# The down product of the last two chunks by seven half-size products, with an order of its own for the last chunk and its stores over two queues

## The chip, the cores and the metric

The kernel runs on one core of one Trainium2 chip. The metric is the device time of one execution in microseconds, the median of several runs; lower is better.

## What is computed

The reference runs a recurrent attention block ("rwkv7 goose") over 4 batches of 8 heads, 768 time steps and 40 channels, and hands its output, 3072 tokens of 320 features, to a feed-forward block:

```
y[t] = r[t] @ state
state = state * w[t] - outer(state @ a[t], b[t]) + outer(v[t], k[t])
...
h = x @ w_in                                  # 3072 x 320 by 320 x 2048
g = h * (1.0 / (1.0 + np.exp(-1.702 * h)))
return g @ w_out                              # 3072 x 2048 by 2048 x 320
```

All of it is float32. The change lies in the last line, the down product `g @ w_out`, and only in the part of it that belongs to the last 512 of the 3072 tokens.

## The kernel before

The 768 time steps are cut into 12 chunks of 64. A chunk has two units, one for each pair of batches, so there are 24 units of 128 tokens. For each unit the recurrence runs in a chunked form: cumulative decays (`ps_cum`, `ps_cumc`), a triangular system whose inverse is built in levels (`ps_N`, `ps_level`, `ps_Q`, `ps_T`), its solution (`ps_B`, `ps_X`), and the outputs and the new state (`ps_y`, then `zr`, and `x` by `decayed`). The unit's output `x` is written to a DRAM tile (`x_dram`, `part_with`) and read back in another layout (`xT_all`, `get_back`).

When both units of a chunk are there, `mlp(c)` runs the feed-forward block on the chunk's 256 tokens:

- **Up** (`up`, tiles `ps_up`): four groups q, each of 2048/4 = 512 hidden features. A group is 10 tasks of four matmuls with 256 columns.
- **Gelu** (`gelu`): one ScalarE instruction for each group, from a PSUM pair of banks into a tile `g`. Four `g` tiles exist.
- **Down** (`down(p)`, tiles `ps_down`): for each of the chunk's two units, 8 tasks `part(m)` of eight matmuls with 320 columns. The 64 tokens of a batch are the stationary operand, rows of `w_out` the moving one. Each half of the hidden features adds up in a bank of its own, so the result is a copy of one bank into `ob` and then an addition of the other (128 x 320 each), and after that two stores on SP's queue, one for each batch.

Every matmul takes a 64 x 64 quarter of the array; four quarters are issued in turn (`QUARTERS`). A float32 matmul of the program shows as two instructions in the profile. All matmuls carry the line of the helper `mm` (L300 in the profile of before), so they are told apart by tile.

The order is written out by hand, as one string `ORDER`. `plan.add` collects 2700 tasks, each with the engines it may run on, what it reads and writes, and for PSUM work a pair of banks. `ORDER` lists them: `2697d2` is task 2697 on VectorE with bank pair 2; p is TensorE, a ScalarE, d VectorE, g GpSimd, s a DMA on SP's queue. Four bank pairs exist. Each engine runs its own tasks in the listed order and waits where a task's inputs are not there. The recurrence of later chunks is woven between the up and down tasks of earlier ones, and the list ends with the up and down tasks of chunk 11 alone.

Of the kernel before, what the change touches and what calls it, by code (L numbers as in the profile page):

```python
# [58 lines left out]
class Plan:  # L59
# [29 lines left out]
    def listed(self, text):  # L89

        assert len(text.split()) == len(self.tasks)
        table, out, done = "exp", [], set()
        for one in text.split():
            e = next(e for e in ENGINES if ENGINES[e] in one)
            n, bank = one.split(ENGINES[e])
            t = self.tasks[int(n)]
            assert e in t.engines and t.after <= done and (e == "SP" or (t.pair is None) == (not bank))
            t.engine, t.bank = e, int(bank or 0)
            if e == "ACT" and t.table:
                t.load, table = t.table != table, t.table  # L100
            done.add(t)
            out.append(t)
        return out
# [4 lines left out]
0s 8s 26s 5s 7s 9s 3a 6s 87p0 88p1 24s 89a1 1s 2s 12s 102a 95d 100p2 90a0 93d 158a 101d2 98p3 96g 10s 94d 17s 97g 16s 99d3  # L108
103p1 4a 11s 132p0 104a1 105d1 142p2 143p3 133a0 106d 130p1 14s 144a3 13s 107p0 15s 18s 151g 108a0 109d0 51s 131a1 110p3 27s
149g 150d 111a3 112d3 159p0 156p1 145a2 161d0 160a0 152g 113p3 345s 92a 162d 25s 153d 114a3 163p2 42s 115d3 34s 19a 274s 264p0  # L110
165d2 265p3 164a2 22d 266a3 166p2 20d 273s 21d 33s 43s 167a2 154p3 168d2 23g 35s 28a 157d1 116p2 155d3 169p1 117a2 118d2 267a0
279d 63s 280g 119p3 277s 171d1 36s 44s 123a3 120d3 343s 125d3 121a 278g 124d3 29d 287a 126p2 170a1 288p0 127a2 30d 172p1 479s
122a3 31d 289a0 128p2 54s 173a1 45s 129d2 32g 62s 174d1 134p3 37a 290d0 175p2 344s 135d3 180a2 146s 178a2 275s 176d2 136p1
179a2 38d 181a2 39d 177a 282g 276s 291d 91s 138a1 182p0 188p3 281d 183a0 186p2 139d 137a1 283p0 187a2 184p1 189a3 40d 140s
292p2 46a 60s 284d0 41g 285p3 185d1 148a 286d3 190p0 293a2 294d2 334p1 335p3 357a 191d0 141s 268g 147s 336a3 315d 192p2 47d
337a1 348d 316p0 194a2 346s 295p3 349d 61s 317a0 195g 347s 358p1 296a3 297d3 360d1 318a0 298p3 271a 361d 319p0 338g 300d3 196s
193a2 320a0 355p2 385d 270s 48d 299a3 362p0 356d2 351g 301p3 363a0 364d0 350g 386p2 197s 302d3 365p0 387a2 269s 352g 359a1
303d3 388a2 323p1 367d0 366a0 321p3 49d 324a1 304p2 322a3 478s 325d1 50g 353p0 309a2 470p3 354d0 209p1 307a2 210p1 310a2 305d2
211p1 308a2 272d 198p0 341a 199p0 72s 212p1 70s 64a 200p0 340s 368p2 52s 342d 339s 69s 201p0 369a2 202p0 370d2 203p0 471a
213p1 65d 214p1 389p2 66d 472a3 483g 204p0 390a2 560s 371p3 67d 306a 53s 215p1 71s 482s 216p1 372a3 217p1 476a 220p2 373d3 68g  # L120
218p1 221p2 477d 219a1 205p0 222p2 206p0 223p2 224p2 78s 559s 207p0 55a 311p3 225p2 79s 312d3 80s 226p2 208a0 58d 313p1 374p3
314d1 227p2 56d 379a3 228p2 229p2 57d 326p0 230a2 59g 393p1 327d0 378a3 391p2 394a1 375d3 231p0 558s 392d2 376a 232p0 233p0
395d1 81s 73a 234p0 480s 381p2 235p0 474s 328p1 475s 382a2 74d 377a3 485d 380a3 236p0 75d 481s 492a 242p2 486d 243p2 82a 76d
484d 77g 383p3 237p0 384d3 244p2 329d1 330d1 488p3 473d 238p0 531d 245p2 487g 246p2 489d3 85d 532p1 708s 239p0 533a1 396p3
331d 534a1 240p0 247p2 397d3 332s 241a0 562s 535p1 83d 490p3 536a1 84d 398p0 706s 572a 491d3 86g 550p1 253p3 399d0 551a 555s
400d0 561s 333s 254p3 401d 255p3 552a1 564d 493p0 402s 556a 567g 570p1 554s 494d0 248p2 705s 563d 566g 249p2 495d0 498d 256p3
571d1 565g 403s 250a2 496a0 251d2 696p1 497g 557d 539p0 252s 537p2 257p3 538a2 704s 540d0 701s 258p3 553d 611d 697a 499d 573p2
259p3 576a2 574d2 784s 710d 700s 260p3 787s 541d0 575d2 404p0 578d 261a3 577g 405p0 579d 698a1 568p2 711g 500p1 406p0 569d2
501a1 407p0 262d3 580p2 702a 502d1 263s 408p0 582d2 409p0 503d 410p0 583d 504a 612p3 411p0 584g 613d3 412p0 614d3 413p0 505p1
709d 414a0 426p3 506d1 427p3 428p3 507d1 429p3 699d 581d2 430p3 615p1 703d 431p3 616a1 785s 585p0 432p3 508d 586a0 433p3 587d0  # L130
434p3 509a 588d 435p3 589d 448p2 436a3 510p1 590p0 511a1 449p2 592d0 591a0 512d1 415p3 513d 416p3 593d 514a 417p3 594g 418p3
515p0 419p3 516a0 517d0 595p1 518d 420p3 596a1 597d1 421p3 598d 422p3 519a 599d 423p3 424p3 520p0 425a3 437p1 521d0 438p1
523d0 522g 439p1 524d0 440p1 525d0 441p1 442p1 526d0 527p3 718p0 528a3 443p1 719d0 929s 444p1 720d0 529p3 445p1 721d0 446p1
530d3 600p0 723d 447a1 542p3 722d 724g 603d0 605a0 619p1 604d0 543d3 450p2 620a1 606d0 544p3 621d1 601d0 602d 617p1 707s 546d3
451p2 618a1 783s 712d 547g 713d 607p0 725p1 608a0 452p2 609p0 453p2 548s 610d0 932s 454p2 727d1 726d1 622p0 728d 545d3 729a
775p1 455p2 623d0 780s 776a 549s 756d 730p3 624p0 456d2 457d2 731d3 458s 459p2 777a1 778g 732d3 786s 788g 781a 779s 626d0
460p2 625d0 627g 733d 795p1 835d 734a 461p2 735p3 791g 462p2 628s 736a3 796d1 737d3 716p0 792g 738d 463p2 782d 739g 1011s
920p1 757p3 925s 464p2 717d0 758a3 629s 759a3 790d 465p2 740p0 789d 466p2 741a0 742d0 921a 797p3 467d2 760p0 1008s 468d2 800a3
923d 652p2 469s 761d0 922a1 653p2 926a 930s 798d3 714p1 799d3 654p2 924s 802d 801g 655p2 934d 803a 656p2 836p0 657p2 715d1
658p2 659p2 837d0 762p3 838d0 927d 660p2 763a3 661p2 764p1 662a2 743d 630p0 744d 928s 631p0 632p0 765d1 804p3 766d1 633p0  # L140
805a3 806d3 634p0 807d 635p0 808a 745p2 636p0 748d2 637p0 749d2 839p1 933g 750d2 638p0 840a1 1009s 751d2 639p0 809p3 746d2
935g 640a0 641p1 810d3 642p1 793p2 747a 811d3 674p0 812d 794d2 813a 752p3 643p1 753a3 814p2 644p1 815a2 816d2 754p3 645p1
755d3 646p1 817d 647p1 818a 767p2 841p3 768d2 648p1 842a3 649p1 819p2 650p1 820a2 821d2 769p3 822d 651a1 823d 675p0 771d3 931s
770d3 772g 824p2 936d 676p0 827a2 828a2 942p1 829a2 677p0 1153s 830a2 937d 945a1 773s 663p3 825d2 664p3 943d1 1156s 826a 665p3
944d1 999p2 947d 946g 666p3 1000a 1004s 980d 940p1 948g 667p3 941d1 668p3 774s 669p3 670p3 831p1 671p3 1001a2 1002d 1003s
832d1 672p3 1005a 1013d 678p0 673a3 1006d 833p2 843p1 679p0 834d2 1007s 844d1 938p2 845d1 680p0 939d2 846p3 681p0 847d3 949p1
# [102 lines left out]
def rwkv7_gelu_quick(ctx: ExitStack, tc: tile.TileContext, time_d, v_d, w_d, wc_d, ak_d, b_d, rv_d, w_in, w_out, out):  # L249
    nc = tc.nc  # L250
# [879 lines left out]
```

## Time and profile before

| | us |
|---|---|
| median of 3 runs | 679.55 (676.51 to 680.0) |
| the profiled execution | 682.79 |
| its span | 681.1 |
| what lies around its span | 1.7 |
| TensorE busy in the span | 652.0 |
| VectorE, ScalarE, GpSimd busy | 445.5, 330.7, 176.7 |

The profile's page gives each engine's busy time. The view of windows gives it by stretch, the view of waits says what an engine stood idle for, the chain of waits follows back what ended last, and the timeline lists instructions in order of time, merged where they are alike: start, length from the first start to the last end, engine, line, operation, tiles, shape and count. A matmul's own length (0.38 us for 256 columns) is a latency; several are in flight, so their pace is read from the starts of neighbouring groups.

### The profile page before, as it was taken

Reading aid. Unit: us, or ns where it says so; the run is one execution under the profiler, and the core shown is the slowest. Engines: PE = TensorE matmul, PEld = TensorE weight load, DVE = VectorE, ACT = ScalarE, POOL = GpSimd, SP = SyncE. Lnnn points to the kernel's source line nnn. Section 1 sums busy time; section 2 is a strip of 40 time slices with the busy share of each in tenths; the row PEclk is TensorE's granted clock in tenths of the full one; section 3 lists DMA queues with packets and bytes.
Section 4 is the critical chain, followed back from the end, with each engine's and each line's share of the span. In section 5 each row is a group of like instructions: output and inputs, shape, how many; then the busy total and the mean of one; then the engine's idle time right before and its main releaser. Section 6 shows DMA issues by size and latency. Waiting matters only on the chain.

```text
span 681.1 us, 42181 instructions
## 1 busy us (share of the span) xinstructions
PE 652.0 (96%) x19488; PEld 572.4 (84%) x19488; DVE 445.5 (65%) x906; ACT 330.7 (49%) x688; POOL 176.7 (26%) x204
## 2 busy tenths in 40 slices
PE   5777999999999999999999999999999999999997
PEld 5667888997987788888888898899899799889996
DVE  4687877777867668767776587868556766675001
ACT  4675845544564654664545445455454354252110
POOL 5443444225123123123123211321412421300000
PEclk9788999999999999999999999999999999999999
DMA  7874755205314314432404413513502312200100
GB/s 235 275 244 148 228 158 173 89 14 155 108 50 139 103 45 125 124 108 67 121 23 131 140 34 107 154 33 106 149 29 71 121 51 58 58 13 23 51 12 21
DMA packets 35312, 69.73 MB, mean 102 GB/s; under 512 B 5440, under 2 KB 14656, under 8 KB 35136
## 3 DMA queue, kind: packets, MB, share of 16 engines
q1 hardware_dynamic: 35136, 67.03, 32.8%
q8 instruction: 153, 2.51, 1.6%
q14 instruction: 23, 0.19, 0.1%
HBM read 59.15 MB, written 7.86 MB: 98 GB/s over the span
## 4 chain that ended last, share of the span: by engine, by line
PE 91%; DMA 4%; ACT 1%; DVE 1%; issue 1%; SPq 0%; ACTq 0%; DVEq 0%
PE ps_up L300 31%; PE ps_down L300 30%; PE ps_level L300 9%; PE ps_y L300 5%; PE ps_B L300 4%; PE ps_X L300 2%; PE ps_N L300 2%; PE ps_rz L300 2%; PE ps_RV L300 2%; PE ps_A L300 1%; DMA ak<-in_ak 1%; PE ps_zT L300 1%; PE ps_Q L300 1%; DMA time<-in_time 1%; PE ps_T L300 1%
## 5 line engine op out<-in xcount | busy, mean ns | idle before, releaser
L300 PE MATMUL ps_up<-xT_all,w_sb 64*64 64x256 f32 x3840 | 254.4, 377 | 2.0 <-DMA xT_all<-x_dram 1.1
L300 PE MATMUL ps_down<-w_sb,g 64*64 64x320 f32 x3072 | 240.3, 430 | 1.1 <-issue 0.9
L300 PEld LDWEIGHTS ps_up<-xT_all,w_sb 64*64 64x64 f32 x3840 | 172.9, 133 | 17.7 <-issue 2.5
L300 PEld LDWEIGHTS ps_down<-w_sb,g 64*64 64x64 f32 x3072 | 143.3, 133 | 31.4 <-issue 1.6
L988 ACT ACTIVATE g<-ps_up 128x1024 f32<-128x1024 f32 x48 | 49.1, 1024 | 44.7 <-PE ps_up L300 44.3
L709 POOL TENSOR_TENSOR EX<-ES,quads 128x512 f32<-128x512 f32 x29 | 38.3, 1323 | 115.5 <-DVE ES L702 83.1
L751 ACT COPY W<-ps_level 128x512 f32<-128x512 f32 x56 | 32.7, 585 | 69.1 <-PE ps_level L300 67.4
L300 PEld LDWEIGHTS ps_level<-W,EX 64*64 64x64 f32 x2560 | 59.2, 134 | 5.8 <-DVE T L830 0.2
L300 PE MATMUL ps_level<-W,EX 64*64 64x64 f32 (+1 forms) x2560 | 56.2, 217 | 0.0
L753 DVE TENSOR_TENSOR E<-two,ps_level 128x256 f32<-128x256 f32 x80 | 33.1, 415 | 34.7 <-ACT W L751 30.7
L707 ACT ACTIVATE EX<-ES,quads 128x256 f32<-128x256 f32 x80 | 36.3, 501 | 30.4 <-DVE ES L702 29.9
L619 POOL TENSOR_TENSOR ak<-ak,FT 128x512 f32<-128x512 f32 x16 | 22.0, 1378 | 76.2 <-DMA ak<-in_ak 54.4
L300 PE MATMUL ps_level<-PT,EX 64*64 64x64 f32 (+2 forms) x1280 | 34.9, 244 | 5.7 <-DVE EX L723 4.8
L300 PEld LDWEIGHTS ps_level<-PT,EX 64*64 64x64 f32 x1280 | 32.6, 145 | 8.9 <-DVE EX L723 5.7
L702 DVE STREAM_TRANSPOSE ES<-E 128x256 f32<-128x256 f32 x80 | 35.2, 442 | 4.7 <-DVE E L753 0.5
L300 PE MATMUL ps_y<-M,bh 64*64 64x104 f32 (+1 forms) x768 | 34.8, 247 | 1.3 <-DVE M L907 0.8
L300 PE MATMUL ps_y<-RV,kh 64*64 64x104 f32 (+1 forms) x768 | 34.9, 247 | 0.3 <-DVE EX L723 0.3
L891 ACT COPY B<-ps_B 128x416 f32<-128x416 f32 (+1 forms) x34 | 16.5, 492 | 33.5 <-PE ps_B L300 33.2
L300 PEld LDWEIGHTS ps_y<-RV,kh 64*64 64x64 f32 x768 | 28.9, 133 | 2.0 <-DVE M L907 0.5
L907 DVE TENSOR_TENSOR M<-ps_X,later 128x832 f32<-128x832 f32 (+1 forms) x24 | 23.8, 993 | 9.8 <-PE ps_X L300 9.5
L627 POOL TENSOR_TENSOR kh<-time,G 128x320 f32<-128x320 f32 x18 | 16.2, 902 | 48.4 <-PE ps_y L300 34.4
L300 PEld LDWEIGHTS ps_y<-M,bh 64*64 64x64 f32 x768 | 27.0, 133 | 1.9 <-DVE M L907 1.2
(131 smaller groups left out, 1097.2 us busy)
## 6 DMA issues: line engine op xcount, KB each, us to landing
ak<-in_ak SPq DMA_DIRECT2D x48, 160.0 KB
rv<-in_rv SPq DMA_DIRECT2D x48, 160.0 KB
time<-in_time SPq DMA_DIRECT2D x24, 320.0 KB
xT_all<-x_dram SPq DMA_DIRECT2D x48, 160.0 KB
wc<-in_wc SPq DMA_DIRECT2D x20, 264.0 KB
logw<-in_w SPq DMA_DIRECT2D x24, 160.0 KB
RV<-in_v SPq DMA_DIRECT2D x24, 160.0 KB
b<-in_b SPq DMA_DIRECT2D x48, 80.0 KB
```

The costliest lines, as they stand in the source:

```text
L300: nc.tensor.matmul(o, lhsT, rhs, start=start, stop=True, skip_group_check=True)
L619: plan.add(R, {"DVE": 690.0, "POOL": 1270.0, "sbuf": True}, lambda t: of(t.engine).tensor_mul(ahT(), ahT(), FT_of(i)), reads=T("ak", "FT") ...
L627: plan.add(R + 4, {"POOL": 870.0, "DVE": 490.0, "sbuf": True}, lambda t, n=n, dst=dst: of(t.engine).tensor_mul(dst(i)[:, :, :D], by_head(t ...
L702: plan.add(rank, dve(256), lambda t: nc.vector.transpose(ES(n), source(t)), writes=[key("ES", n, 6)], **reads)
L707: nc.scalar.activation(dst[:, :, h], ES(n), ACT.Copy, scale=quads[:, h, :1])
L709: of(t.engine).tensor_mul(dst, ES(n).unsqueeze(2).to_broadcast([128, 8, 2, 32]), quads.unsqueeze(1).to_broadcast([128, 8, 2, 32]))
L751: plan.add(rank, any2(512), lambda t: copy(t.engine)(tiles_of(W(n + 1)), blocks(psum(t, ""), 64)), writes=[key("W", n + 1, 5)], pair=pair)
L753: plan.add(rank, dve(256), lambda t: nc.vector.tensor_sub(tiles_of(E(n + 1)), every(two32, [128, 2, 4, 32]), blocks(psum(t, ""), 64)[:, :, ...
L891: plan.add(R, any2(4 * wide), lambda t: copy(t.engine)(dst(), some(psum(t, "")[:, :, :208])), writes=[("Bv", i)] if x and c > 0 else T("B" ...
L907: plan.add(R + 1, dve(8 * wide), lambda t: nc.vector.tensor_tensor(M_of(i)[:, :, :wide].rearrange("p (j b) n -> p b j n", b=2), some(psum( ...
L988: plan.add(-45, {"ACT": 1030.0, "table": "gelu"}, lambda t: nc.scalar.activation(g_of(c * NQ + q).rearrange("p m r n -> p r m n"), psum(t, ...
```

## The change

For chunks 10 and 11, `down` is replaced by `fast_down`. The product of a chunk, 256 tokens by 2048 features by 320 outputs, is seen as 2 x 2 blocks: the two units' tokens (p), two halves of the hidden features (s), and two halves of 160 outputs (d). Seven products of blocks take the place of eight, with sums before and after them (Strassen's scheme in Winograd's form):

- `factors()`: four combinations T1 to T4 of the blocks of `w_out`, made once, in two parts each (8 instructions of 128 x 640). They lie in `extra`, the staging tile of the weights.
- `mixed`: four combinations S1 to S4 of the blocks of `g`, in two parts each (8 instructions of 128 x 512 for a chunk), S2 to S4 partly in place of `g`.
- `product_of`: M1 to M7, each in two parts (j) of sixteen matmuls with 160 columns.
- `summed` and `added`: the banks are copied and added into SBUF (160, 320 or 480 columns wide), and combined into the four blocks of the result.
- Chunk 11 has its own order: M1 first, M2 last of all, added in PSUM onto M1, and the store of each block as soon as it is there. Of each pair of its stores one is issued on SP's queue and one on ScalarE's.

Beside this, `g` has six tiles in place of four, and its layout is [2, 4, 128] in place of [2, 2, 256] for all chunks, with the gelu's access patterns to match (the same 1024 elements). A scratch size of the DMA set-up is made smaller. The list `ORDER` is another one: 2736 tasks. Task by task, TensorE's order is the same in both lists for its first 651 tasks, SP's for its first 200, ScalarE's for 297, VectorE's for 512, GpSimd's for 88 (where the first `factors` tasks stand); from there all five differ. Some tasks before that have another bank pair. In number TensorE has 4 tasks fewer, ScalarE 10 fewer, VectorE 33 more, GpSimd 16 more and SP 1 more; in the last chunk all added arithmetic is on VectorE.

The diff without the list and without blank lines:

```diff
+            if e == "SP":
+                t.window = t.bank
...
+    FAST = (10, 11)
...
-                     ... x=1, xT=3, g=4, ob=1), 4)
+                     ... x=1, xT=3, g=6, ob=1, S10=1, S11=1, of=1, n6=1, n7=1), 4)
...
-    g_of = lambda n: buf("g", n, [128, 2, 2, 256])
+    g_of = lambda n: buf("g", n, [128, 2, 4, 128])
...
+    DH = DM // 2
+    S1 = single("S1", [128, 2, 4, 128])
+    T1, T2, T3, T4 = (extra[:, k * PIECE:(k + 1) * PIECE].rearrange("p (j f n) -> p j f n", j=2, f=4) for k in range(4))
+    B11, B12, B21, B22 = (w_out_sb.rearrange("p (j s f d n) -> p j s f d n", j=2, s=2, f=4, d=2)[:, :, s, :, d] for s in BITS for d in BITS)
+    of_fast, new6, new7 = (single(name, [128, n, DH]) for name, n in (("of_fast", 4), ("new6", 3), ("new7", 2)))
+    def light(n):
+        return {"POOL": 270.0 + 2.1 * n, "DVE": 165.0 + 1.03 * n, "sbuf": True}
+    def factors():
+        staged = [("weight", n) for n in range(len(raws))]
+        for dst, a, b, name, reads in ((T1, B12, B11, "T1", staged), (T2, B22, T1, "T2", [("T1", 0)]),
+                                       (T3, B22, B12, "T3", staged), (T4, B21, T2, "T4", [("T2", 0)])):
+            for j in BITS:
+                plan.add(10000, light(640), lambda t, dst=dst, a=a, b=b, j=j: of(t.engine).tensor_sub(dst[:, j], a[:, j], b[:, j]),
+                         reads=reads, writes=[(name, 0)])
+    def fast_down(c):
+        R = 10000 + 100 * c
+        last = c == NU // 2 - 1
+        A11, A21, A12, A22 = (lambda j, s=s, p=p: g_of(c * NQ + 2 * j + s)[:, p] for s in BITS for p in BITS)
+        g = lambda j, *which: [("g", c * NQ + 2 * j + s) for s in which]
+        T = lambda *names: [(name, c) for name in names]
+        s1 = lambda j: S1[:, j]
+        def mixed(j, name, dst, a, b, reads, writes, add=False):
+            def go(t):
+                (of(t.engine).tensor_add if add else of(t.engine).tensor_sub)(dst(j), a(j), b(j))
+            plan.add(-44, light(512), go, reads=reads, writes=writes + [(f"{name}{j}", c)])
+        def product_of(pair, n, at, a, b, j, reads, first=True):
+            def go(t):
+                po = psum(t, "ps_fast")
+                for f in range(4):
+                    for r, h in QUARTERS:
+                        mm(po[HALF[h], r, at * DH:(at + 1) * DH], a(j)[HALF[r], 2 * (f % 2) + f // 2, h * 64:h * 64 + 64], b[HALF[r], j, f],
+                           first and at == 0 and j == 0 and f == 0)
+            plan.add(R + 20 + n, pe((4, DH)), go, reads=reads, writes=T(f"M{n}{j}"), pair=("down", (c, pair)), most=1)
+        def summed(pair, n, dst, key, name, free=()):
+            flat = lambda: dst().rearrange("p k n -> p (k n)")
+            plan.add(-45, any2(n * DH), lambda t: copy(t.engine)(flat(), psum(t, "")[:, 0, :n * DH]), reads=T(*free), writes=T(key), pair=("down", (c, pair)))
+            plan.add(-45, dve(n * DH), lambda t: nc.vector.tensor_add(flat(), flat(), psum(t, "")[:, 1, :n * DH]),
+                     reads=T(key), writes=T(name), pair=("down", (c, pair)))
+        def added(dst, a, b, n, reads, uses, name):
+            plan.add(-45, light(n * DH), lambda t: of(t.engine).tensor_add(dst(), a(), b()), reads=T(*reads), uses=T(*uses), writes=T(name))
+        def store(p, reads, some=slice(0, 2)):
+            n = some.stop - some.start
+            def go(t):
+                for b in BITS:
+                    o = (2 * p + b) * S + c * C
+                    queue = nc.scalar if last and b else nc.sync
+                    queue.dma_start(out[o:o + C, some.start * DH:some.stop * DH], of_fast[HALF[b], 2 * p + some.start:2 * p + some.stop].rearrange("p k n -> p (k n)"))
+            plan.add(-100, {"SP": 700.0}, go, reads=T(*reads), uses=T("of"), size=64 * DM * 4 * n)
+        M1, M2, M4, M5, M6, M7 = ((x, y, z) for x, y, z in (
+            (A11, B11, lambda j: g(j, 0) + [("weight", NQ + 2 * j)]), (A12, B21, lambda j: g(j, 1) + [("weight", NQ + 2 * j + 1)]),
+            (A22, T4, lambda j: g(j, 1) + [("T4", 0)]), (s1, T1, lambda j: T(f"S1{j}") + [("T1", 0)]),
+            (A11, T2, lambda j: g(j, 0) + T(f"S2{j}") + [("T2", 0)]), (A21, T3, lambda j: g(j, 0) + T(f"S3{j}") + [("T3", 0)])))
+        def products(pair, *some):
+            for n, at, (a, b, reads), j in some:
+                product_of(pair, n, at, a, b, j, reads(j))
+        for j in BITS:
+            mixed(j, "A", s1, A21, A22, g(j, 0, 1), T(f"S1{j}"), add=True)
+            mixed(j, "S3", A21, A11, A21, g(j, 0) + T(f"A{j}"), [])
+        if last:
+            products(0, *((1, 0, M1, j) for j in BITS))
+        else:
+            products(0, *((n, n % 2, M, j) for j in BITS for n, M in ((2, M2), (1, M1))))
+        S4 = s1 if last else A12
+        for j in BITS:
+            mixed(j, "S2", A11, s1, A11, g(j, 0) + T(f"S1{j}", f"S3{j}", f"M1{j}"), [])
+            if not last:
+                mixed(j, "S4", S4, A12, A11, g(j, 0, 1) + T(f"S2{j}", f"M2{j}"), [])
+        if not last:
+            summed(0, 2, lambda: of_fast[:, :2], "of", "M21")
+            added(lambda: of_fast[:, 0], lambda: of_fast[:, 0], lambda: of_fast[:, 1], 1, ["M21"], ["of"], "C11")
+        else:
+            summed(0, 1, lambda: of_fast[:, 1:2], "of", "M21")
+        products(1, *((4, 0, M4, j) for j in BITS), *((5, 1, M5, j) for j in BITS), *((6, 2, M6, j) for j in BITS))
+        if last:
+            for j in BITS:
+                mixed(j, "S4", S4, A12, A11, g(j, 0, 1) + T(f"S2{j}", f"M5{j}"), [])
+        summed(1, 3, lambda: new6, "n6", "M456")
+        added(lambda: new6[:, 2], lambda: new6[:, 2], lambda: of_fast[:, 1], 1, ["M456", "M21"], ["of", "n6"], "U")
+        added(lambda: new6[:, :2], lambda: new6[:, :2], lambda: new6[:, 2].unsqueeze(1).to_broadcast([128, 2, DH]), 2, ["U"], ["n6"], "XW")
+        M3 = S4, B22, lambda j: g(j, 1) + T(f"S4{j}") + [("weight", NQ + 2 * j + 1)]
+        products(2, *((n, at, M, j) for j in BITS for n, at, M in ((7, 0, M7), (3, 1, M3))))
+        summed(2, 2, lambda: new7, "n7", "M73")
+        added(lambda: of_fast[:, 1], lambda: new6[:, 1], lambda: new7[:, 1], 1, ["XW", "M73", "U"] + ([] if last else ["C11"]), ["of", "n6", "n7"], "C12")
+        added(lambda: of_fast[:, 2:], lambda: new6[:, :2], lambda: new7[:, 0].unsqueeze(1).to_broadcast([128, 2, DH]), 2, ["XW", "M73"], ["of", "n6", "n7"], "C2")
+        if last:
+            store(0, ["C12"], slice(1, 2))
+            store(1, ["C2"])
+            for j in BITS:
+                a, b, reads = M2
+                product_of(0, 2, 0, a, b, j, reads(j) + T("M21"), first=False)
+            summed(0, 1, lambda: of_fast[:, 0:1], "half", "C11", free=["M21"])
+            store(0, ["C11"], slice(0, 1))
+        else:
+            store(0, ["C11", "C12"])
+            store(1, ["C2"])
...
-                g_of(c * NQ + q).rearrange("p m r n -> p r m n"), psum(t, "").rearrange("p r (m n) -> p r m n", m=2),
+                g_of(c * NQ + q).rearrange("p q b n -> p b q n"), psum(t, "").rearrange("p r (m q n) -> p (r m) q n", m=2, q=2),
...
-                    po, g = psum(t, "ps_down"), g_of(c * NQ + m // 2)[:, m % 2]
+                    po, g = psum(t, "ps_down"), g_of(c * NQ + m // 2)[:, p]
...
-                            o = p * 128 + b * 64
-                            mm(po[HALF[b], r, :DM], g[HALF[r], f % 2, o:o + 64], w_out_sb[HALF[r], f * DM:(f + 1) * DM], f == 0)
+                            mm(po[HALF[b], r, :DM], g[HALF[r], 2 * (f % 2) + m % 2, b * 64:b * 64 + 64], w_out_sb[HALF[r], f * DM:(f + 1) * DM], f == 0)
...
-        for p in BITS:
-            down(p)
+        if c in FAST:
+            fast_down(c)
+        else:
+            for p in BITS:
+                down(p)
...
+            if i // 2 == min(FAST):
+                factors()
...
-    nc = bacc.Bacc("TRN2", target_bir_lowering=False, num_devices=1)
+    nc = bacc.Bacc("TRN2", target_bir_lowering=False, num_devices=1, dynamic_dma_scratch_size=2048)
```

The end of the new list, from chunk 11's last up tasks on (2688 to 2697 are up tasks, 2665, 2676, 2687, 2698 gelu; 2699 to 2702 S1 and S3, 2703 and 2704 M1, 2705 and 2706 S2, 2707 and 2708 drain M1, 2709 to 2714 M4, M5, M6, 2715 and 2716 S4, 2717 to 2720 their sums, 2721 to 2724 M7 and M3, 2725 to 2728 sums, 2729, 2730 and 2735 stores, 2731 and 2732 M2, 2733 and 2734 its drain):

```
2691p2 2692p2 2686p1 2693p2 2687a1 2694p2 2695p2 2696p2 2676a0 2697p2 2703p3 2698a2 2704p3 2709p1 2707d3 2708d3 2699d
2701d 2700d 2710p1 2702d 2711p1 2705d 2712p1 2706d 2721p2 2716d 2715d 2713p1 2714p1 2722p2 2717d1 2718d1 2723p2 2719d
2720d 2724p2 2725d2 2726d2 2727d 2728d 2729s 2730s 2731p3 2732p3 2733d3 2734d3 2735s
```

More of the change, by code (lines that the diff above doesn't have):

```diff
@@ L112 @@
[L112 to L115, printed above, removed]
```

274 lines of the change are left out of this document (140 added, 134 removed).

## The prediction

> **What bounds the kernel now.** I read the page first, then windows, TensorE's waits, the timeline and the chain of the end.
>
> The page's busy times; then two windows (length; busy us and instructions of PE, PEld, DVE, ACT, POOL; granted clock; DMA share; GB/s):
>
> ```profile
> PE 652.0 (96%) x19488; PEld 572.4 (84%) x19488; DVE 445.5 (65%) x906; ACT 330.7 (49%) x688; POOL 176.7 (26%) x204
> ```
> ```profile
> 100.00:400.00 300.00, 299.33 (x9198) 253.26 (x9194) 216.22 (x455) 158.94 (x315) 80.40 (x84) 1.00 0.34 100
> 400.00:660.00 260.00, 258.64 (x7582) 234.08 (x7577) 156.97 (x340) 108.11 (x224) 50.25 (x55) 1.00 0.23 69
> ```
>
> TensorE stands idle for 0.67 and 1.36 us in these stretches, at the full granted clock; no other engine is busy for three quarters of them. Busy may still mean slow, so the pace is needed. Timeline, an early piece and the end, and the chain of the end:
>
> ```profile
> 50.32 0.52 PE L300 MATMUL ps_cum<-logw,edges 64*64 64x160 f32 x8
> 50.59 0.61 PE L300 MATMUL ps_cumc<-edges,logw 64*64 64x65 f32 x26
> ```
> ```profile
> 657.59 4.64 PE L300 MATMUL ps_up<-xT_all,w_sb 64*64 64x256 f32 x80
> 661.91 14.32 PE L300 MATMUL ps_down<-w_sb,g 64*64 64x320 f32 x208
> ```
> ```profile
> 662.23 14.02 PE ps_down L300 x208
> 676.25 0.02 issue
> 676.27 0.50 DVE ob L1012
> 676.77 0.02 issue
> 676.79 0.49 DVE ob L1014
> ```
>
> 80 up instructions take 661.91 - 657.59 = 4.32 us, 54.0 ns each; the 208 down instructions take 14.02 us, 67.4 ns each. From 639.58 the chain holds 320 up and 288 down instructions and nothing else of TensorE: 320 x 54.0 + 288 x 67.4 = 36.7 us, and 639.58 to 676.25 is 36.67. So the end is set by the columns that TensorE streams; matmul time taken away there shortens the span one for one, as long as no new wait comes.
>
> **The change part by part.**
>
> *Products.* A chunk's down is 256 instructions (16 parts x 8 matmuls x 2): 256 x 67.4 = 17.25 us. The seven products are 448 instructions (14 parts x 16 x 2) of 160 columns. Their pace: `ps_cum` above has that width, 8 instructions from 50.32 to 50.59, 33.8 ns each; a line through 256 and 320 columns (13.4 ns for 64 columns) gives 54.0 - 96 x 0.209 = 33.9; half of 67.4 is 33.7. I take 34.0, so a part is 32 x 34.0 = 1.09 us and a chunk 15.23 us. That is 2.02 us less, 4.04 for two chunks. The bounds 33.7 and 34.3 move this by 0.3 either way; a far worse pace is a rival below.
>
> *The tail behind TensorE.* Before: copy and addition of 320 columns, 0.50 + 0.02 + 0.49, then two stores from one queue, 677.31 to 678.42:
>
> ```profile
> 677.31 1.11 SPq L1011 DMA_DIRECT2D out<-ob  x2
> ```
>
> After: M2 is the last product, and its copy and addition are 160 wide. From 0.49 for 320 columns and 0.69 for 512 (the x of the VectorE groups below) a column costs 1.04 ns, so 0.32 each, 0.34 less in all. One store stands on SP's queue and one on ScalarE's, so one issue of about 0.59 (SP's median; 0.47 to 1.24 are its extremes) in place of 1.11. No DMA is issued by ScalarE before; I take SP's price, as the nearest. That makes -0.86, between -1.0 and -0.2. The landing behind it stays.
>
> *The work round the products.* 16 `mixed` (512 columns), 8 `factors` (640), 9 `added` and 14 drain instructions come, 8 drains go. The prices (least, median and greatest ns, from the view of single lines):
>
> ```profile
> L709 DVE TENSOR_TENSOR EX<-ES,quads x31: 649/691/845, 117.2 to 613.6; 128x512 f32<-128x512 f32 x31
> L709 POOL TENSOR_TENSOR EX<-ES,quads x29: 1272/1280/1679, 126.2 to 599.7; 128x512 f32<-128x512 f32 x29
> L619 DVE TENSOR_TENSOR ak<-ak,FT x8: 650/708/1697, 7.5 to 470.3; 128x512 f32<-128x512 f32 x8
> ```
>
> None is on TensorE, so each costs nothing as long as its consumer finds it done. The places:
>
> - Four `factors` on GpSimd stand behind an EX and ahead of `ak<-ak,FT`, which in the trace are these (0.87 us for 320 columns and 1.28 for 512 make 1.5 for 640, so 6.2 us in a hole of 9.7 that a load leaves; without it, `ak` and ps_A behind it would be 6.2 us late):
>
> ```profile
> 377.36 1.28 POOL L709 TENSOR_TENSOR EX<-ES,quads 128x512 f32<-128x512 f32 x1 [2.90 <-DVE ES L702]
> 388.34 1.27 POOL L619 TENSOR_TENSOR ak<-ak,FT 128x512 f32<-128x512 f32 x1 [9.70 <-DMA ak<-in_ak]
> ```
>
> - The last x before chunk 11's up. Before: y is read at 628.86, x ends at 630.48, its write is issued at once, and the read back was issued only at 635.36 behind a store; up still starts on time.
>
> ```profile
> 628.86 0.69 DVE L943 TENSOR_TENSOR zr<-ps_y,zr 128x512 f32<-128x512 f32 x1 [2.39 <-PE ps_y L300]
> 629.58 0.90 DVE L953 TENSOR_TENSOR x<-zr,FT 128x128 f32<-128x128 f32 x4
> ```
> ```profile
> 625.88 0.67 SPq L963 DMA_DIRECT2D x_dram<-x  x2
> 628.05 1.11 SPq L967 DMA_DIRECT2D xT_all<-x_dram  x2
> 630.51 0.66 SPq L963 DMA_DIRECT2D x_dram<-x  x2
> 634.13 1.13 SPq L1011 DMA_DIRECT2D out<-ob  x2
> 635.36 1.19 SPq L967 DMA_DIRECT2D xT_all<-x_dram  x2
> ```
>
>   After, TensorE has nine product parts between that y and up, 9 x 1.09 = 9.8 us (before, the down stretch from 628.5 to 639.3, 10.8). On SP's queue: write from 1.65 (counted from the reading of y) to 2.3, a store to 3.4, unit 22's read back to 4.6, unit 23's to 5.8 (its own write landed by 1.65 + 2.17 = 3.8); landing within 2.7, since before it took at most 636.55 to 639.26. So 8.5 against 9.8: no wait, 1.3 to spare.
> - Chunk 11's sums. M5 needs S1, which stands on VectorE behind the two drains of M1. From the end of up: M1 is done at 2.18 + 0.30 (latency: 14.32 against 14.02), drains 0.64, S1 0.69, so 3.8; TensorE comes to M5 after four parts, at 4.36. VectorE then makes a sum each 0.65 us, TensorE eats one each 1.09, so the margin of 0.5 grows. S4 must wait for M5 (it overwrites S1): M5 ends at 6.84, S4 is there by 8.2, M3 comes at 9.8. Gelu: the group that M4 needs ends about when up does, 2.2 us early. All 0; a missing cover costs what is late beyond these margins.
>
> *The other order, six g tiles.* Two thirds of it stand as before. In 400:660 TensorE can at best win back the idle 1.36; at worst 100 us of it run like 60 to 100 us, where windows show 38.08 busy of 40, a loss of 1.92 in 40, so 4.8. The nearest row, 100:400, lost 0.67; I take 0 change. The gelu's new pattern moves the same 1024 elements; its 1.02 us are off the path.
>
> **Sum.** -4.04 - 0.86 = -4.9 us. The profiled execution's 682.79 (span 681.1 and 1.7 around it) becomes 677.9. It lies 3.24 above the median of 679.55, so the median becomes 674.65, which I write as **674.7**.
>
> **The rivals.**
>
> 1. *The new order eats it.* The order from the 652nd TensorE task on is static, and 39 more instructions stand on other engines ahead of the tail or in it; any of them late stops TensorE, since it may not pass a waiting task. For: 1.4 us of idle exist in that stretch already, 1.1 of them in one wait for `xT_all`. Against: margins as worked out above. At 1.6 to 4.8 us lost: 676.3 to 679.5.
> 2. *Slower: narrow products do not hide their weight loads.* 896 product instructions replace 512. At 64 columns the pace cannot be below the loads' own: 32 `ps_level` instructions start over 0.46 us, 14.4 ns each. If that came on top of the streaming, a part would run at 34.0 + 14.4 = 48.4, 896 x 14.4 = 12.9 us more, and the time would be 687.6. It decides from 34.0 + 4.9 / 0.896 = 39.5 ns on. Against: `ps_cum` at 33.8, and the line through 256 and 320 columns, which leaves no room for loads. In the Trainium skill, "TensorE: Matmul & The Clock Gate", Part 3, The mechanism, weight loads overlap matmuls in flight only where the row group differs; here the third quarter of four shares the first's rows, and by that rule some of the load would show. At 256 and 320 columns this trace shows none.
> 3. *GpSimd holds VectorE up.* The rows above show an addition of two SBUF tensors stretched from 0.65 to 1.70 us; the new GpSimd work is 6 `factors` and 3 `mixed`. If each stretches one VectorE instruction by 1.05 and a third reach TensorE: 3.2 us, 677.9. Against: nearly all are in holes. The Trainium skill, "SBUF — State Buffer", SBUF: two separate sides, says of the port pair that these two engines share that it is "an **exclusive lock**, not a bandwidth split"; by that rule the second one waits for the whole of the first, as the 1.70 bears out.
>
> **How the numbers follow.** Forecast 0.70, rival 1 0.17, rival 2 0.06, rival 3 0.07. The forecast's own range is 673 to 676.2 (0.3 for the pace, 1.4 of idle won back, 0.7 of the tail, the spread of a median whose runs lie 3.5 apart). The whole range reaches into rivals 1 and 3 and leaves rival 2 out: 672.6 to 678.9. A change of 0.5%, 3.4 us, is about what this kernel's measurement can tell: faster is below 676.2. The forecast lies there with about 0.93, rivals 1 and 3 hardly: 0.67. Slower, above 682.9, is rival 2 and a rest: 0.07. Same: 0.26.
>
> **What would show it.** Right: chunk 11's product parts at 1.09 us, 32 instructions each, without a gap; up of chunk 11 directly behind M6; the last drain at 0.32 + 0.32 and two stores issued side by side; TensorE's waits behind 100 us near 2 us in all. Wrong: a pace above 39 ns, a wait of `ps_fast` for VectorE, of `ps_up` for `xT_all`, or new waits from 400 us on that add up to over 1.5 us.

## The result: 3.1 us faster, of 4.9 forecast

| | before | after |
|---|---|---|
| median, us (runs) | 678.62 (22) | 675.75 (22) |
| the profiled execution, us | 682.79 | 678.24 |
| its span, us | 681.1 | 676.5 |

The ratio after to before is 0.9954, 95% interval 0.9935 to 0.9974. On the first median of before, 679.55, that is 3.1 us less, between 1.8 and 4.4 (the two medians in the table differ by 2.9). The two profiled spans differ by 4.6 us.

The lines of after that answer to those of before: the busy times of the page, then the two windows (length; busy us and instructions of PE, PEld, DVE, ACT, POOL; granted clock; DMA share; GB/s):

```profile
PE 646.4 (96%) x19872; PEld 564.1 (83%) x19872; DVE 466.6 (69%) x937; ACT 321.8 (48%) x671; POOL 194.6 (29%) x220
```
```profile
100.00:400.00 300.00, 299.78 (x9228) 259.44 (x9224) 221.94 (x455) 158.23 (x314) 87.98 (x89) 1.00 0.34 100
400.00:660.00 260.00, 258.67 (x7863) 225.14 (x7864) 165.00 (x359) 101.09 (x210) 63.45 (x67) 1.00 0.23 69
```

TensorE is idle for 0.22 and 1.33 us (before 0.67 and 1.36): it still sets the time, and the new order has brought hardly any new idling into these stretches. VectorE has 21 us more to do, GpSimd 18, and both lie beside it. The end of the chain of waits in after (start, length, what held the end back):

```profile
635.77 4.03 DMA xT_all<-x_dram
639.79 0.14 issue
639.93 17.20 PE ps_up L305 x313
657.13 0.14 PE ps_fast L305
657.27 0.14 PE ps_up L305 x2
657.40 15.25 PE ps_fast L305 x445
672.66 0.02 issue
672.68 0.34 DVE of_fast L1024
673.02 0.02 issue
673.04 0.32 DVE of_fast L1025
```

The products of chunk 11 take 15.25 us without a gap (the ordinary down: 17.25), and the last two VectorE instructions 0.34 and 0.32. But the chain now holds a DMA. TensorE's timeline there, and its waits behind 100 us (us in total, times, longest):

```profile
632.28 1.36 PE L305 MATMUL ps_fast<-extra,g 64*64 64x160 f32 x32
633.37 1.36 PE L305 MATMUL ps_fast<-w_sb,g 64*64 64x160 f32 x32
...
638.80 0.59 PE L305 MATMUL ps_up<-xT_all,w_sb 64*64 64x256 f32 x2
639.93 2.39 PE L305 MATMUL ps_up<-xT_all,w_sb 64*64 64x256 f32 x40 [0.54 <-DMA xT_all<-x_dram]
```
```profile
PE ps_up L305 <- DMA xT_all<-x_dram: 0.5, 1, 0.5
PE ps_A L305 <- issue: 0.5, 1, 0.5
PE ps_T L305 <- DVE QT L823: 0.2, 1, 0.2
PE ps_up L305 <- PE ps_rz L305: 0.2, 1, 0.2
```

Two parts of chunk 10 start 1.09 us apart, as forecast. Then two up instructions run, and the third waits: two instructions of 54 ns from 638.80 on end at 638.91, the next starts at 639.93, so 1.0 us is lost. (The view of waits books 0.5, since a matmul's modelled end reaches into the gap.) The reason stands on VectorE and SP's queue:

```profile
629.33 0.69 DVE L948 TENSOR_TENSOR zr<-ps_y,zr 128x512 f32<-128x512 f32 x1 [2.30 <-PE ps_y L305]
630.11 0.90 DVE L958 TENSOR_TENSOR x<-zr,FT 128x128 f32<-128x128 f32 x4
```
```profile
632.07 1.11 SPq L1129 DMA_DIRECT2D out<-ob  x2
633.29 3.07 SPq L972 DMA_DIRECT2D xT_all<-x_dram  x4
```

y is read at 629.33; the four read backs are issued from 633.29 to 636.36, behind a store of chunk 9; the last one starts at 635.77 and lands at 639.79, 10.5 us behind the reading of y.

### The profile page after: what moved, and what is told of

The parts are those of the page before. It is cut to its first block, busy times and chain, and to the rows that moved or that the text cites. A ratio compares the mean times of both kernels' runs of the same rounds, so it can differ in the third digit from the quotient of the medians.

```text
span 676.5 us, 42974 instructions
## 1 busy us (share of the span) xinstructions
PE 646.4 (96%) x19872; PEld 564.1 (83%) x19872; DVE 466.6 (69%) x937; ACT 321.8 (48%) x671; POOL 194.6 (29%) x220
## 4 chain that ended last, share of the span: by engine, by line
PE 91%; DVE 3%; DMA 2%; ACT 1%; issue 1%; SPq 1%; DVEq 0%; ACTq 0%
PE ps_up L305 31%; PE ps_down L305 26%; PE ps_level L305 10%; PE ps_y L305 5%; PE ps_B L305 5%; PE ps_fast L305 3%; PE ps_X L305 3%; PE ps_N L305 2%; PE ps_rz L305 2%; PE ps_A L305 2%; PE ps_RV L305 2%; DMA logw<-in_w 1%; PE ps_zT L305 1%; DVE EX L728 1%; PE ps_cum L305 1%
## 5 line engine op out<-in xcount | busy, mean ns | idle before, releaser
L305 PE MATMUL ps_up<-xT_all,w_sb 64*64 64x256 f32 x3840 | 249.7, 377 | 1.0 <-DMA xT_all<-x_dram 0.5
L305 PE MATMUL ps_down<-w_sb,g 64*64 64x320 f32 x2560 | 199.5, 430 | 0.0
L305 PEld LDWEIGHTS ps_up<-xT_all,w_sb 64*64 64x64 f32 x3840 | 170.0, 133 | 18.6 <-issue 2.1
L305 PEld LDWEIGHTS ps_down<-w_sb,g 64*64 64x64 f32 x2560 | 108.4, 133 | 32.7
L758 DVE TENSOR_TENSOR E<-two,ps_level 128x256 f32<-128x256 f32 x80 | 33.2, 416 | 39.5 <-ACT W L756 22.8
L712 ACT ACTIVATE EX<-ES,quads 128x256 f32<-128x256 f32 x74 | 33.6, 501 | 35.6 <-DVE ES L707 35.2
L714 POOL TENSOR_TENSOR T<-ES,quads 128x512 f32<-128x512 f32 x9 | 11.5, 1275 | 64.5 <-DVE ES L707 64.5
L802 ACT COPY Tc<-ps_level 32x64 f32<-32x64 f32 x92 | 18.5, 201 | 22.2 <-PE ps_level L305 12.9
L305 PEld LDWEIGHTS ps_y<-RV,kh 64*64 64x64 f32 x768 | 27.3, 135 | 2.0
```

The source lines that it names most:

```text
L305: nc.tensor.matmul(o, lhsT, rhs, start=start, stop=True, skip_group_check=True)
L712: nc.scalar.activation(dst[:, :, h], ES(n), ACT.Copy, scale=quads[:, h, :1])
L714: of(t.engine).tensor_mul(dst, ES(n).unsqueeze(2).to_broadcast([128, 8, 2, 32]), quads.unsqueeze(1).to_broadcast([128, 8, 2, 32]))
L758: plan.add(rank, dve(256), lambda t: nc.vector.tensor_sub(tiles_of(E(n + 1)), every(two32, [128, 2, 4, 32]), blocks(psum(t, ""), 64)[:, :, ...
L802: copy(t.engine)(dst, src[:, u, :, f])
```

## The experiments

In this table, "first y" is the start of the first VectorE instruction that reads `ps_y`, "last copy" the start of the last copy out of PSUM, both from the timeline, and "to the end" the rest of the span, and "clock" the mean granted clock over all runs of a kernel. Each group of runs was measured beside runs of before of its own, with medians of 679.63 (e1 to e4), 680.34 (e5 to e8), 678.22 (e9 to e11) and 681.13 (e12); so across groups the ratios compare, the medians only roughly. The last three columns come from one profiled execution of each kernel. The forecast spoke of the stretch behind the first y; the start ahead of it turned out to be a matter of its own.

| kernel | median, us | ratio to before, 95% interval | clock | first y | first y to last copy | to the end |
|---|---|---|---|---|---|---|
| before | | | 0.993 | 97.95 | 578.32 | 4.81 |
| after | 675.75 | 0.9954, 0.9935 to 0.9974 | 0.992 | 99.33 | 573.35 | 3.84 |
| e1 | 676.00 | 0.9947, 0.9925 to 0.9969 | 0.991 | 100.04 | 573.35 | 3.84 |
| e2 | 680.81 | 1.0017, 0.9994 to 1.0040 | 0.991 | 94.77 | 576.25 | 4.81 |
| e3 | 676.12 | 0.9938, 0.9913 to 0.9962 | 0.993 | 99.28 | 572.26 | 3.83 |
| e4 | 677.26 | 0.9960, 0.9936 to 0.9983 | 0.991 | 95.21 | 573.59 | 5.19 |
| e5 | 695.64 | 1.0208, 1.0167 to 1.0248 | 0.999 | 106.30 | 582.34 | 4.31 |
| e6 | 691.55 | 1.0172, 1.0133 to 1.0211 | 0.998 | 105.44 | 578.92 | 3.84 |
| e7 | 694.10 | 1.0174, 1.0130 to 1.0218 | 0.997 | 105.83 | 581.72 | 3.82 |
| e8 | 692.79 | 1.0181, 1.0144 to 1.0219 | 0.998 | 105.58 | 578.42 | 4.78 |
| e9 | 677.25 | 0.9991, 0.9967 to 1.0015 | 0.998 | 99.26 | 572.85 | 3.82 |
| e10 | 675.78 | 0.9975, 0.9951 to 0.9999 | 0.999 | 98.77 | 571.77 | 3.82 |
| e11 | 680.51 | 1.0035, 1.0005 to 1.0066 | 0.998 | 100.65 | 575.76 | 4.81 |
| e12 | 686.63 | 1.0081, 1.0053 to 1.0109 | 0.997 | 105.49 | 581.05 | 3.81 |

The letters of the theories hold within one group of runs (e1 to e4, e5 to e8, and so on). In e3, Theory C is the queue; from e5 on it is the clock.

**e1, e2: is it the start's banks?** The first 1372 entries of both lists hold the same tasks, interleaved differently and with other bank pairs. In after, TensorE's 3000th instruction came at 120.08 us, in before at 118.70. e1 is after with before's first 1372 entries (bank pairs behind them renamed to match), e2 is before with after's. The start of e1's edit, and its first entries behind the seam:

```diff
-0s 8s 26s 5s 7s 9s 3a 6s 87p0 88p1 24s 1s 89a1 2s 102a 95d 90a0 93d 158a 12s 100p2 98p3 ...
+0s 8s 26s 5s 7s 9s 3a 6s 87p0 88p1 24s 89a1 1s 2s 12s 102a 95d 100p2 90a0 93d 158a 101d2 ...
...
-1301s 1476p2 1507d 1592p0 1405d 1137p1 1477a2 ...
+1301s 1476p1 1507d 1592p0 1405d 1137p3 1477a1 ...
```

> The changed kernel, but its first 1372 listed tasks (no product of the change among them) have the bank pairs of the list before, and the rest of its list has its pairs renamed to fit. Theory A (the other choice of banks in the first microseconds costs what is missing between the forecast of -4.9 us and the measured -2.9): TensorE's busy time in the first 100 us comes back from 75.3 to about 77.8 us, and the time falls by 1.5 to 2.5 us against the changed kernel, to some 4.5 to 5 us under the kernel before. Theory B (the start differs from run to run, whatever the banks): the busy time of the first 100 us lies anywhere between 75 and 78, and the time is the changed kernel's within 1 us, some 3 us under the kernel before.

> The kernel before, but its first 1372 listed tasks have the bank pairs of the changed list. Theory A: TensorE's busy time in the first 100 us falls from 77.8 to about 75.3 us and the kernel gets 1.5 to 2.5 us slower than before. Theory B: the same time as before within 1 us.

e1's time is after's (676.00), its first y even later, and TensorE is busy 75.1 us of its first 100, not the 77.8 of Theory A. e2 is 1.2 us above the runs of before beside it, between the marks of the two theories, with an interval of the ratio that holds 1; TensorE is busy 75.7 us there, and its first y is the earliest of all. So A falls by e1, and e2 alone decides nothing. The first y lies anywhere from 94.8 to 100.0 among the six profiles of before, after and e1 to e4 and does not go with either list. Behind the first y, e2 needs 2.1 us less than before's own profile, which had a 1.1 us wait for `xT_all` at 493 us and 0.5 of `issue`. In e2, e8 and e11, which share before's list from entry 1373 on, up does not wait there; so part of the 5.0 us between the two profiles belongs to that one execution of before.

**e3: the read backs first.**

```diff
-... 2475d 2653s 2482g 2263s 2497p1
-2580s 2498p1 2483d 2654s 2484d3 ...
+... 2475d 2580s 2653s 2482g 2497p1
+2498p1 2483d 2654s 2263s 2484d3 ...
```

(2580 and 2654 read x of units 22 and 23 back, 2653 writes unit 23's, 2263 stores a block of chunk 9.)

> The changed kernel with two entries of SP's queue moved: the read back of unit 22's x stands ahead of the write of unit 23's x, and chunk 9's last store stands behind the read back of unit 23. Theory C (chunk 11's up waits for its x because a store and two read backs stand in line on SP's queue, 0.86 us lost): the last read back is issued about 2 us earlier, the wait of ps_up for xT_all near 640 us is gone, and the time falls by 0.9 us against the changed kernel. Rival: the read back's flight sets it, not the queue; then up still waits for about 0.5 us or more.

The view of waits of e3 behind 100 us, complete, and SP's queue:

```profile
PE ps_T L305 <- DVE QT L823: 0.2, 1, 0.2
PE ps_up L305 <- PE ps_rz L305: 0.2, 1, 0.2
```
```profile
633.12 1.17 SPq L972 DMA_DIRECT2D xT_all<-x_dram  x2
634.33 1.24 SPq L1129 DMA_DIRECT2D out<-ob  x2
```

Unit 23's read back is issued by 634.29, 2.1 us earlier than in after, and the wait is gone. First y to last copy is 572.26 against 573.35: the wait had cost 1.1 us. The median does not show it (676.12); the ratio is the lowest of all twelve, 4.2 us below before, but its interval, 3.3 us wide, overlaps that of after.

**e4: the last stores on one queue.**

```diff
-                    queue = nc.scalar if last and b else nc.sync
+                    queue = nc.sync
```

> The changed kernel with all stores on SP's queue. By the sum of the prediction the second queue is worth one issue, 0.5 us: the last pair of stores takes 1.0 to 1.1 us to issue in place of 0.55, and the end lies 0.5 us later behind the last addition. Rival (the issue is hidden behind the landing of the stores ahead of it, or ScalarE's queue is slower to issue): no difference behind the last addition, or an end that is earlier with one queue.

The end is 1.35 us longer (5.19 against 3.84), more than twice the 0.5 expected. The median is 1.5 us above after's, but the ratios (0.9960 and 0.9954) do not tell the two apart. The timeline of e4 for SP's queue, then that of after for SP's and for ScalarE's:

```profile
668.03 3.66 SPq L1038 DMA_DIRECT2D out<-of_fast  x6
```
```profile
671.90 1.95 SPq L1038 DMA_DIRECT2D out<-of_fast  x3
```
```profile
671.91 2.05 ACTq L1038 DMA_DIRECT2D out<-of_fast  x3
```

Chunk 11 has three pairs of stores, not one. On one queue six issues take 3.66 us, 0.61 each, from 668.03 to 671.69: the last pair stands behind the first two and is through 2.2 us after the last addition (it starts at 669.16 and ends at 669.48). On two queues three each are through at 673.96, 0.6 us after it (673.36). Without the second queue the end is longer than before's 4.81.

**e5 to e8: does the clock set the start?** In all six profiles so far the clock was granted at half for 3.4 to 13.6 us between 19 and 67 us, in pieces of 3.4 us, and in after's 22 runs a higher clock went with a shorter time (correlation -0.58). The first y goes with it: the two profiles with 3.4 us at half clock (e2, e4) read it at 94.8 and 95.2, the four with 13.6 us between 98.0 and 100.0. That is no proof that the clock is the cause. Matmuls of zeros, overwritten later, fill the gaps in e5; e6 has some ahead of the first gaps too; e7 is e6 with e3's order; e8 is e2 with e6's fillers. The edit of e5 (the keys are tasks, the values numbers of calls):

```diff
+    idle = {110: 20, 113: 10, 166: 8, 116: 10, 169: 24, 126: 22, 134: 8, 182: 18, 190: 14, 298: 16, 319: 10}
     for t in tasks:
+        for k in range(idle.get(plan.tasks.index(t), 0)):
+            r, h = QUARTERS[k % 4]
+            mm(psum(t, "ps_warm")[HALF[h], r, :256], warm[HALF[r], :64], warm[HALF[r]], True)
         t.fn(t)
```

> The kernel after, with 160 matmuls of 256 columns of zeros added in eleven places between 18 and 64 us where TensorE waits (8 to 24 in a place, at 54.0 ns each less than the idle time shown there; their results are overwritten). Theory C (the clock is granted at half for 3.4 us after a stretch of 3.4 us in which TensorE had little to do, and how many such stretches there are changes from execution to execution; this, and no step of the change, makes the spread and 1 to 2 us of what is missing): half-clock stretches between 25 and 67 us fall from 3 or 4 units of 3.4 us to at most 1, the mean granted clock of the runs rises from 0.992 to 0.996 or more, the median falls by 1.5 to 3 us to 672.7 to 674.2. Rival D (the start is paced by loads and VectorE whatever the clock): median 675 to 677, no change, or later by what the added matmuls delay.

> The same and 54 more such matmuls ahead of the first three places where TensorE waits (up to 12 us). Theory C: the clock, granted in full only from about 16 to 19 us on in all profiles so far, is granted by 8 to 12 us; the matmuls up to there run at the full pace, and the 3000th TensorE instruction of the kernel itself comes 2 to 5 us earlier than in the kernel after (120.08): median 671 to 673. Rival D: as in the run before, 675 to 677.

> The last run with the store of chunk 9 behind the last read backs on SP's queue, so that up of chunk 11 does not wait for x. Every theory: the wait of ps_up for xT_all (0.5 to 0.9 us) is gone and the median is 0.5 to 0.9 below the run before; Theory C: 670.2 to 672.4, the least of all kernels here; Rival D: 674.3 to 676.

> The kernel before (both last chunks by the ordinary product) with the first 1372 entries of the new order and the same 214 added matmuls as in e6. It takes the clock out of the comparison: its time less that of e6 is what the change behind the start is worth. Forecast's terms as the traces measured them: products 4.0 and tail 1.0, less 0.9 for the wait for x: 4.1 (3.5 to 5). Theory C further: its own median 675.5 to 677.5, below the kernel before's 679.6. Theory E (the new order or the added work on VectorE and GpSimd costs something between the start and chunk 10 that no wait shows): less than 3.2 between the two.

All four missed by 14 to 19 us, on the slow side of every theory. e7 came out 2.5 us above e6, where 0.5 to 0.9 less was expected. One cause is plain: a call is two instructions, so that e5's fillers took 17.3 us (320 times 54.0 ns) in gaps of about 10; first y came 7 us late. The clock did rise, to 0.997 and more. The other cause is new: from first y to the last copy e5 needs 9.0 us more than after, where nothing was added. Its waits for `issue` behind 112 us are many (before and after had 0.5 each behind 100):

```profile
PE ps_level L305 <- issue: 2.4, 4, 0.8
PE ps_up L305 <- issue: 0.9, 1, 0.9
PE ps_B L305 <- issue: 0.8, 1, 0.8
PE ps_zT L305 <- issue: 0.5, 1, 0.5
PE ps_T L305 <- issue: 0.5, 2, 0.3
```

These waits lie close behind packets of the DMA queue that the page calls `instruction`. In the trace's single records of e5, TensorE's next instruction starts over 0.2 us late at 20 places behind the first y; 15 of them, 9.2 us in all, lie 2.0 to 3.1 us behind the start of such a packet of 16 KB.

The place in TensorE's own list says more. After has 40035 recorded TensorE instructions (weight loads, matmuls, semaphores) and 156 packets of 16 KB, e5 has 40675 and 159: one packet for about 256 instructions. Numbered in order, and counted modulo 256, 15 of e5's 20 late starts stand between 190 and 204, which is 15 places out of 256. So they come at one fixed point of a block of 256 instructions. Of all other late starts over 0.3 us in after, e3 to e7, e9, e10 and e12, three recur in every one of these kernels at the same three matmuls (0.3 to 0.6 us each, whatever their place among the 256), and the rest are waits of `ps_up` for `xT_all`.

At that point e5 has 15 late starts of 9.0 us in all, e6 13 of 5.7, e7 17 of 8.2, e8 4 of 2.3; after has 3 of 1.2, e3 4 of 1.1, e10 2 of 1.0, e11 2 of 0.9. So TensorE now and then waits for its own instructions, and how often depends on the kernel; why e5 to e7 are hit so often stays open. That also spoils the pair e6 and e8, whose medians differ by 1.2 us, as Theory E would have it: behind the first y e6 is 0.5 us longer, where 4 less were expected, and 3.4 us more of such waits are most of the difference.

**e9 to e11: a third of the fillers.** e9 is after, e10 e3's order, e11 e2, each with

```diff
+    idle = {110: 6, 116: 3, 169: 12, 126: 10, 182: 8, 190: 5, 298: 6, 319: 4}
```

> As e5, with 108 added matmul instructions in place of 320: in the trace of e5 each added call came out as two instructions of 54 ns, so that the added work was 17.3 us where the gaps held some 10. Now it is 108 x 54.0 = 5.8 us in eight gaps that hold 10.7. Theory C (half-clock stretches follow stretches with little work for TensorE, and cost time): mean granted clock 0.995 or more over the runs (0.992 in the kernel after), at most one half-clock stretch of 3.4 us behind 25 us, median 673 to 675, below the kernel after's 675.75 by 1 to 3. Theory D (the start is paced by loads and the other engines; the clock is no cost): median 675 to 677 although the clock is higher. Theory F (what made e5 to e8 slow was not the added work alone but waits for instructions, `issue`, that added instructions bring): median over 677 and more than 2 us of `issue` waits behind 100 us.

> The last run with the store of chunk 9 behind the last read backs. 0.5 to 0.9 us less than e9 by every theory; Theory C 672.2 to 674.4, the least median of all kernels here.

> The kernel before with the first 1372 entries of the new order and the same 108 added instructions as e9. e11 less e9 is what the change behind the start is worth: 4.1 us by the terms that the traces measured (products 4.0 and tail 1.0, less 0.9 for the wait for x), within 1.5 either way; from the first reading of y to the end of the span the two profiles differ by 3.9 to 5.9, as before and after did.

The clock is 0.996 or more in every one of e9's twelve runs, and the median is no lower than after's: 677.25 against 675.75. By the ratios, e9 and e10 are both 2.5 us longer than their kernels without fillers (0.9991 against 0.9954, 0.9975 against 0.9938), with intervals that still touch. Theory C's gain did not come; e9 lies just above Theory D's 677. The windows of after and then of e9 for the start:

```profile
0.00:50.00 50.00, 29.75 (x952) 26.41 (x952) 30.32 (x47) 26.48 (x72) 22.02 (x50) 0.90 0.79 251
50.00:100.00 50.00, 45.60 (x1483) 40.76 (x1484) 39.66 (x60) 35.99 (x77) 21.15 (x15) 0.97 0.59 181
```
```profile
0.00:50.00 50.00, 33.49 (x1105) 28.62 (x1107) 32.50 (x55) 27.99 (x75) 22.20 (x51) 1.00 0.81 251
50.00:100.00 50.00, 45.92 (x1445) 41.27 (x1439) 36.29 (x53) 34.22 (x74) 20.48 (x15) 0.97 0.58 180
```

In the first 50 us the clock goes from 0.90 to 1.00 and TensorE is busy 3.7 us longer, much of it with fillers; the first y stays at 99.3. Either the clock costs nothing there, or what it gives back goes into the 5.8 us of fillers. The three kernels do give clean stretches behind the first y, without waits for instructions over 0.4 us in the view of waits: e11 less e10 is 575.76 - 571.77 = 3.99, e9 less e10 1.08. By the medians e11 less e9 is 3.3 (4.1 expected, within 1.5), and e10 lies 1.5 below e9 (0.5 to 0.9 expected).

**e12: three gaps alone**, on e3's order: `{169: 9, 126: 9, 182: 6}`.

> The order of e3 with 48 added matmul instructions (2.6 us at 54.0 ns) in three of the gaps alone (2.03, 1.95 and 1.54 us long, at 31 to 49 us). Theory C (the half-clock stretches cost time, and in e9 the gain was given back to the 5.8 us of added work): clock 0.995 or more, the first y read at 95 to 97 us, as in the two profiles with only 3.4 us at half clock (94.8 and 95.2), and median 672.5 to 674.5. Theory D (the start is paced by something else, the clock costs nothing that a median shows): first y read at 98 to 100 and median 675.5 to 677, as e3's 676.1, although the clock is higher.

Neither: the median is 686.63, with 48 added instructions. By the ratios that is 9.7 us above e3, which has none, and 7.2 above e10, which has 108. The profiled execution is the longest of its twelve runs (692.06, 5.4 above their median), so it shows more than a usual run. In it half-clock stretches are back (13.6 us before 70 us and 3.4 more at 97), and TensorE waits even among the last products:

```profile
PE ps_fast L305 <- issue: 1.6, 2, 1.2
PE ps_down L305 <- issue: 1.5, 2, 0.9
PE ps_y L305 <- issue: 0.5, 2, 0.3
```

17 late starts, 8.1 us, stand at that fixed point. Theory F asked for over 2 us of `issue` behind 100 us: e5 (5.4 us), e7 (3.4) and this one profile of e12 (3.8) have it, e6 nearly (1.9), e9 to e11 do not (0.4 at most), and the cost does not grow with the number of fillers. What is left open: whether the half clock costs time by itself, and which number of instructions ahead makes TensorE wait at the packets. The lowest ratio of all stays e3's.

## Why the prediction was right

The direction and the range were right, and 674.7 lies 1.7 below what the ratio gives (676.4). The mechanism was right in its two terms, products and tail. Of its own signs of being wrong one came all the same, a wait of `ps_up` for `xT_all`: a step said to cost nothing cost 1.1 us. The forecast's own range, 673 to 676.2, holds the median and just misses 676.4, which also lies at the edge of rival 1's 676.3 to 679.5; the time alone would not have told the two apart, the traces do. That the number still came so near, with a wait of 1.1 us left out, is in part luck. By its steps:

- **Products, -4.04: right.** 15.25 us for chunk 11 in the chain, and 3.99 us between e11 and e10 and between e2 and e3 (576.25 - 572.26), for both chunks. Each kernel of these pairs has one profile.
- **Tail, -0.86: right in sum; what the second queue is worth was too low.** 4.81 becomes 3.84, so -0.97: 0.33 in the copy and the addition (0.34 forecast), 0.64 behind them (0.52 forecast). But e4 shows that the second queue is worth 1.35, more than the whole term: the prediction priced one issue saved, and did not count that on one queue the pieces before the last hold it up.
- **"So 8.5 against 9.8: no wait, 1.3 to spare": wrong.** It was 10.5 (639.79 - 629.33) against 9.6 (638.91 - 629.33). The queue reached the end of the issues at 7.0, not 5.8: the write of x took 1.00 us in place of 0.65, the read backs 3.07 for four in place of 2.4, the first of them 1.16. The landing took 3.4 behind the last issue (636.36 to 639.79), where 2.7 had been called a bound from one row of before. Cost: 1.1 us by e3 and e10. Before's own trace spoke against both figures. Its read backs took 0.45 to 1.70 us each to issue, and in its chain one that was issued from 488.74 to 489.33 lands 3.8 us later, and TensorE waits for it:

```profile
488.74 4.43 DMA xT_all<-x_dram
493.17 0.04 issue
493.21 2.88 PE ps_up L300 x49
```

  A margin of 1.3 made of medians, on such a queue, was no margin.
- **The other places said to be covered: right.** The four factors took 6.91 us on GpSimd (6.2 forecast), and `ak` behind them still waited for its load:

```profile
377.98 1.28 POOL L714 TENSOR_TENSOR EX<-ES,quads 128x512 f32<-128x512 f32 x1 [2.90 <-DVE ES L707]
379.22 6.91 POOL L994 TENSOR_TENSOR extra<-w_sb 128x640 f32<-128x640 f32 x4
389.10 1.27 POOL L624 TENSOR_TENSOR ak<-ak,FT 128x512 f32<-128x512 f32 x1 [2.97 <-DMA ak<-in_ak]
```

  Chunk 11's sums kept ahead of TensorE: no gap in its products.
- **New order and idle, 0: right but for the x above.** In 400:660 the idle time is 1.33 us in place of 1.36, but it is not the same: before's wait at 493 is gone, the one at 639.9 is new.
- **Summed again with what was measured:** -3.99 - 0.97 + 1.1 = -3.9 us, inside the interval of 1.8 to 4.4. The 0.8 between -3.9 and -3.1 is not explained, and is too small for these intervals to show; the start's first y, which no step of the change explains, moved by 5 us from profile to profile.
- **Rivals.** Rival 1, at 0.17, named the right kind of wait ("1.1 of them in one wait for `xT_all`"), but the one that it quoted is before's at 493 us, which is gone in after; the new one stands at 639.9, costs 1.1 us, below its 1.6, and comes from one place of a store on SP's queue, as e3 shows. Rival 2 fell: 32 instructions in 1.09 us are 34.0 ns, below 39.5. By the rule in the Trainium skill, "TensorE: Matmul & The Clock Gate", Part 3, The mechanism, that weight loads overlap matmuls in flight only where the row group differs, some of the loads would have shown in quarters that share one; at 160 columns none does. (The same section of the Trainium skill also lets a load go ahead into a background weight buffer; no run here tells whether that is the reason.) Rival 3: no wait of TensorE for VectorE over 0.2 us behind 100 us; nothing reached it.

## What to carry to other kernels

Where TensorE sets the time, work taken from it comes back one for one (3.99 us of 4.04 here), and neighbours' busy time is free as long as each consumer's margin holds; so spend the care on the margins, and make those on a DMA queue from the slowest issues and landings in the trace, not from the medians. When a transfer feeds the bounding engine, put it ahead of the stores on its queue; and when a last result is stored in pieces, count all the pieces' issues on a queue, not the last one's. Change nothing ahead of a stretch that is to be compared: 48 to 428 added TensorE instructions near the start lengthened the time from first y to last copy by up to 9 us (in the profiles of e5 and e12).

## What was not expected of the hardware

- **TensorE waits for its instructions.** The instruction queue moves 16 KB at a time, one packet for about 256 of TensorE's instructions. In e12 thirteen starts behind the first y are over 0.3 us late; ten of them, up to 1.45 us, stand at place 192 to 195 of 256 and lie 2.2 to 2.9 us behind the start of such a packet, and the other three, 0.31 to 0.54 us late, are those that come at the same matmuls in all kernels with the change. The Trainium skill, "Runtime: NRT & Kernel Launch", Instruction fetch mechanics, gives the block of 16 KiB, 256 instructions, and calls the crossing "mostly hidden"; in the kernels without fillers and in e8 to e11 the trace agrees (0.9 to 2.3 us in some 575), in e5 to e7 and e12 it does not (5.7 to 9.0). The fixed place shows that these waits belong to the blocks; what makes a block late was not tested.
- **The clock is granted at half inside the start of a busy kernel**, in pieces of 3.4 us, and in every unfilled profile from 36 to 37 us on, close to a wait of TensorE of 1.9 to 2.5 us (in after two of 2.0, between 31.7 and 37.1). Filling the gaps with 108 instructions took the mean clock from 0.992 to 0.998 and gave no time back; whether the half clock costs time there was not separated from what the fillers cost.
- **An issue on ScalarE's queue costs a little more than on SP's:** the last three took 0.55, 0.76 and 0.55 us there, and 0.47, 0.54 and 0.47 on SP's.
